# A fused linear-attention and SwiGLU block: tiles 0 to 2 enter K and Q unscaled, GpSimd normalises them, and x 6 to 13 are loaded without a wait

## The chip, the cores and the metric

One core of a Trainium2 chip. The metric is the device time of one execution in microseconds (us), the median of several. Engines are named as in the profile: PE is TensorE (matmuls and transposes), DVE is VectorE, ACT is ScalarE, POOL is GpSimd, SP is SyncE, which here only issues DMAs. Each engine has its own instruction list and works through it in order; a wait at its head holds everything behind it. ACT and SP also have a DMA queue each. SBUF holds 128 partitions; PSUM has eight banks of 128 x 512 f32.

## The reference

x has 2048 rows of 512 bf16 values. `xn` is x less its row mean over its row deviation. The result is `x + A(xn) + B(xn)`:

```
q, k, v = heads of xn @ wqkv            (32 heads of 16)
phi(t)  = where(t > 0, t + 1, exp(t)) + 1e-6
kv = phi(k)^T v,  z = sum of phi(k)     (per head, over all rows)
A  = (phi(q) kv / (phi(q) z + 1e-6)) @ wo
B  = (silu(xn @ w_gate) * (xn @ w_up)) @ w_down      (w_gate, w_up: 512 x 1792)
```

## The kernel before, in words

The rows are cut into 16 tiles of 128. All loads, weights and results lie in SBUF. A small class, `_Prog`, keeps one list per engine. `K.op` appends one entry, with the names that it reads and writes, and puts in the waits that these names need; `K.dma` does it for a DMA. So the order of the calls in the file is the order on each engine.

Stage 1 (lines 537 to 642) goes over the tiles. For tile t: `bns` and `agg` (DVE) give mean and variance; `rstd_pow` gives 1/deviation, an add of 1e-5 (`vpe`, on DVE for the tiles in `VD`, else on POOL) and a pow on POOL; `xn_dve` (DVE) normalises into `xn_sb`; a transpose brings it to `xnT`, from tile 3 on as a DMA transpose on SP's queue; `kproj` and `qproj` (PE, four matmuls of 512 columns each, into banks 2(t mod 2) and 2(t mod 2) + 1); `exp_k`, `exp_q` (ACT, exp of K, exp and copy of Q); `feat_k` (DVE: `clip` to phi's range, then `maxadd`, and on POOL a running sum `zsum`); `gtacc` (PE) accumulates `xn^T phi(k)` into banks 4 to 7. v is never formed: `gtacc`'s sum is multiplied by v's weights later.

The first tiles have their own code. Tile 0 enters the matmuls as x less its mean (`xc_half`, two halves, transposed by PE through PSUM and copied by ACT to `xcT`); since K and Q are linear, rstd is applied as the `scale` of the ACT evictions (`first_ek`, `first_pk`, `first_eq`, `first_pq`), and `first_feat` (DVE) adds relu and clipped exp, both from SBUF. Tiles 1 and 2 are normalised on DVE and transposed by PE. `fill` puts matmuls on constants on PE between these steps.

x 0 to 5 and the weights of K and Q are loaded at the start on both queues (lines 240 to 250). x 6 and 7 are issued on SP behind a wait for the weights of Q (line 251); x 8 to 15 in pairs by `xn(3)`, `xn(5)`, `xn(6)` and `xn(7)`, each right behind that tile's DMA transpose on SP (lines 528 to 535). The later weights follow on SP in the loop at t = 10.

Stage 2 (`ffn`, 56 steps of gate and up matmuls, line 656) has the attention's end woven in, and stage 3 the output matmuls (lines 828 and 839). Neither is touched.

Of the kernel before, what the change touches and what calls it, by code (L numbers as in the profile page):

```python
# [10 lines left out]
P = 128  # L11
S = 2048
D = 512
# [95 lines left out]
def bass_parallel_sum__linear_attn_block__swiglu_ffn__prompt_kernel(  # L109
# [16 lines left out]
    with contextlib.ExitStack() as es:  # L126
# [7 lines left out]
        xc_sb = sb("xc_sb", [D])  # L134
        xcT = sb("xcT", [NDC, P])
        kpos = sb("kpos", [D], f32)
# [103 lines left out]
        xload("sp", sp, 0, 1)  # L240
        xload("sp", sp, 1, 1)
        wqkv_load("act", act, "wk", 1, 0, 2)
        wqkv_load("sp", sp, "wk", 1, 2, 2)
        xload("act", act, 2, 1)
        wqkv_load("act", act, "wq", 0, 0, 2)
        wqkv_load("sp", sp, "wq", 0, 2, 1)
        wqkv_load("act", act, "wq", 0, 3, 1)
        xload("act", act, 3, 1)
        xload("sp", sp, 4, 1)
        xload("act", act, 5, 1)  # L250
        xload("sp", sp, 6, 2, [("wq", 0), ("wq", 2), ("wq", 3)])
# [51 lines left out]
        VD = (1, 2, 3)  # L303
# [34 lines left out]
        def xc_half(h):  # L338
            K.op(
                "dve",  # L340
                lambda: dve.tensor_scalar(
                    out=xc_sb[:, h * HD:(h + 1) * HD], in0=x_sb[:, 0, h * HD:(h + 1) * HD],
                    scalar1=mv[:, 0, 0:1], scalar2=None, op0=ALU.subtract,
                ),
                r=[("x", 0), ("mv", 0)], w=[("xc", h)],
            )

        def xn_half(t, h):
            K.op(
                "dve",  # L350
                lambda: dve.tensor_scalar(
                    out=xn_sb[:, t, h * HD:(h + 1) * HD], in0=x_sb[:, t, h * HD:(h + 1) * HD],
                    scalar1=mv[:, t, 0:1], scalar2=rstd[:, t:t + 1], op0=ALU.subtract, op1=ALU.mult,
                ),
                r=[("x", t), ("mv", t), ("rstd", t)], w=[("xnh", t, h)] + ([("xn", t)] if h else []),
            )

        def transpose_half(src, key, dst, wkeys, b, h):
# [5 lines left out]
                        tb[:, c, :], src[:, (2 * h + c) * P:(2 * h + c + 1) * P], ident[:, :],  # L364
# [3 lines left out]
                r=[key, ("ident",)], w=[bk(b)],  # L368
# [3 lines left out]
                lambda: act.activation(dst[:, 2 * h:2 * h + 2, :], tb, ACT.Copy),  # L372
                r=[bk(b)], w=wkeys,
# [10 lines left out]
        def proj(t, b, lo, wname):  # L384
# [9 lines left out]
                r=[("xnT", t), (wname, 0), (wname, 2)] + ([(wname, 3)] if wname == "wq" else []), w=[bk(b)],  # L394
            )

        def proj_part(src, key, b, lo, wname, h):
# [4 lines left out]
                        banks[b], src[:, c, :], wqkv_sb[:, c, lo:lo + D],  # L402
# [4 lines left out]
                r=[key, (wname, 2 * h)] + ([(wname, 3)] if wname == "wq" and h else []), w=[bk(b)],  # L407
# [48 lines left out]
        def first_ek():  # L456
            K.op(
                "act", lambda: act.activation(ek[:, 0, :], banks[kb(0)], ACT.Exp, scale=rstd[:, 0:1]),
                r=[bk(kb(0)), ("rstd", 0)], w=[("ek", 0)],
            )  # L460

        def first_pk():
            K.op(
                "act", lambda: act.activation(kpos[:, :], banks[kb(0)], ACT.Relu, scale=rstd[:, 0:1]),
                r=[bk(kb(0)), ("rstd", 0)], w=[("kpos",)],
            )

        def first_eq():
            K.op(
                "act", lambda: act.activation(eq[:, 0, :], banks[qb(0)], ACT.Exp, scale=rstd[:, 0:1]),  # L470
                r=[bk(qb(0)), ("rstd", 0)], w=[("eq", 0)],
            )

        def first_pq():
            K.op(
                "act", lambda: act.activation(pkq[:, 0, 1, :], banks[qb(0)], ACT.Identity, scale=rstd[:, 0:1]),
# [459 lines left out]
```

## Time and profile before

| | us |
|---|---|
| median of 3 runs | 212.66 (212.58 to 212.66) |
| profiled execution | 213.16 |
| its span, first to last instruction | 211.9 |
| PE busy in the span | 207.7 (98%) |
| DVE, ACT, POOL busy | 118.9, 68.1, 73.1 |
| K 0's first matmul, line 401 | 5.25 |
| K 3's first matmul, line 388 | 14.10 |
| K 6's first matmul | 22.20 |
| first matmul of stage 2, line 656 | 48.96 |

The granted TensorE clock was 1.000. A row of a timeline gives start, length, engine, line, operation, output<-inputs and, in brackets, how long the engine had been idle and what ended that. Lines are those of the kernel before. A group of several instructions shows the time from the first's start to the last's end. "POOL rstd L316" is the pow, "vpe L309" the add in front of it, "pkq L483" `first_feat`, "zacc" the running sum.

### The profile page before, as it was taken

Reading aid. Unit: us, or ns where it says so; the run is one execution under the profiler, and the core shown is the slowest. Engines: PE = TensorE matmul, PEld = TensorE weight load, DVE = VectorE, ACT = ScalarE, POOL = GpSimd, SP = SyncE. Lnnn points to the kernel's source line nnn. Section 1 sums busy time; section 2 is a strip of 40 time slices with the busy share of each in tenths; the row PEclk is TensorE's granted clock in tenths of the full one; section 3 lists DMA queues with packets and bytes.
Section 4 is the critical chain, followed back from the end, with each engine's and each line's share of the span. In section 5 each row is a group of like instructions: output and inputs, shape, how many; then the busy total and the mean of one; then the engine's idle time right before and its main releaser. Section 6 shows DMA issues by size and latency. Waiting matters only on the chain.

```text
span 211.9 us, 2784 instructions
## 1 busy us (share of the span) xinstructions
PE 207.7 (98%) x1001; PEld 95.9 (45%) x1001; DVE 118.9 (56%) x244; ACT 68.1 (32%) x119; POOL 73.1 (35%) x93
## 2 busy tenths in 40 slices
PE   8899999999999999999999999999999999999996
PEld 3344444445444444444444444444444444444454
DVE  3899796533454776546374746464556535374121
ACT  4486666866453332213122312112032213121000
POOL 3368787748022444122140442131414031221100
PEclk9999999999999999999999999999999999999999
DMA  5647634893792011120101011101021010110201
GB/s 182 214 99 125 152 74 86 282 363 102 200 353 57 0 25 25 50 27 25 47 4 50 10 35 33 50 0 50 3 50 25 25 25 28 45 31 26 51 28 50
DMA packets 28623, 16.45 MB, mean 78 GB/s; under 512 B 19136, under 2 KB 27968, under 8 KB 28608
## 3 DMA queue, kind: packets, MB, share of 16 engines
q1 hardware_dynamic: 27488, 15.21, 27.0%
q10 hardware_dynamic: 1120, 1.05, 1.5%
q8 instruction: 8, 0.13, 0.3%
q14 instruction: 7, 0.06, 0.1%
HBM read 9.70 MB, written 2.10 MB: 56 GB/s over the span
## 4 chain that ended last, share of the span: by engine, by line
PE 89%; DMA 5%; DVE 4%; ACTq 1%; issue 0%; ACT 0%
PE psum L656 46%; PE psum L839 23%; PE psum L388 8%; PE psum L828 7%; PE psum L514 4%; DMA x_sb<-in_A_x_dram 3%; DMA xnT<-xn_sb 2%; DVE stats L288 1%; DVE pkq L450 1%; DVE xn_sb L296 1%; PE psum L754 0%; PE psum L777 0%; ACTq L204 0%; DVE ek L441 0%; DVE pkq L483 0%
## 5 line engine op out<-in xcount | busy, mean ns | idle before, releaser
L671 ACT ACTIVATE sg<-psum 128x512 bf16<-128x512 f32 x56 | 33.4, 598 | 106.8 <-PE psum L656 104.9
L656 PE MATMUL psum<-xnT,wg_sb 128*128 128x512 bf16 x224 | 57.5, 379 | 0.0
L656 PE MATMUL psum<-xnT,wu_sb 128*128 128x512 bf16 x224 | 57.5, 379 | 0.0
L786 POOL TENSOR_TENSOR prod<-pkq,zb 128x512 f32<-128x512 bf16 x16 | 18.6, 1161 | 57.8 <-DVE pkq L450 57.8
L656 PEld LDWEIGHTS psum<-xnT,wu_sb 128*128 128x128 bf16 x224 | 21.9, 98 | 26.4
L656 PEld LDWEIGHTS psum<-xnT,wg_sb 128*128 128x128 bf16 x224 | 21.9, 98 | 26.2
L852 DVE TENSOR_TENSOR out_sb<-psum,x_sb 128x512 bf16<-128x512 f32 (+1 forms) x17 | 11.2, 660 | 36.0 <-PE psum L839 36.0
L677 DVE TENSOR_TENSOR pkq<-psum,sg 128x512 bf16<-128x512 f32 x28 | 19.1, 687 | 18.6 <-PE psum L656 14.0
L810 POOL TENSOR_TENSOR pqn<-pkq,rden 128x512 bf16<-128x512 bf16 x16 | 16.9, 1055 | 36.5 <-DVE rden L804 36.5
L388 PE MATMUL psum<-wqkv_sb,xnT 128*128 128x512 bf16 x116 | 27.3, 379 | 0.2 <-DMA xnT<-xn_sb 0.2
L677 DVE TENSOR_TENSOR xn_sb<-psum,sg 128x512 bf16<-128x512 f32 x28 | 18.8, 672 | 14.2 <-PE psum L656 12.6
L839 PE MATMUL psum<-wd_sb,xn_sb 128*128 128x512 bf16 (+1 forms) x126 | 25.7, 355 | 0.0
L839 PE MATMUL psum<-wd_sb,pkq 128*128 128x512 bf16 x112 | 25.5, 379 | 0.0
L506 POOL TENSOR_TENSOR zacc<-zacc,pkq 128x512 f32<-128x512 f32 x15 | 17.3, 1154 | 6.3 <-DVE ek L441 5.7
L839 PEld LDWEIGHTS psum<-wd_sb,xn_sb 128*128 128x128 bf16 x126 | 12.3, 98 | 11.9
L388 PEld LDWEIGHTS psum<-wqkv_sb,xnT 128*128 128x128 bf16 x116 | 11.1, 98 | 13.9 <-ACT eq L430 0.6
L839 PEld LDWEIGHTS psum<-wd_sb,pkq 128*128 128x128 bf16 x112 | 11.0, 98 | 13.2
L828 PE MATMUL psum<-m_sb,eq 128*128 128x512 bf16 (+1 forms) x68 | 16.6, 366 | 0.0
L514 PE MATMUL psum<-pkq,xn_sb 128*128 128x512 bf16 x64 | 16.1, 379 | 0.0
L794 DVE TENSOR_REDUCE den<-prod 128x32 f32<-128x512 f32 x16 | 10.9, 684 | 5.7 <-POOL prod L786 5.7
L288 DVE BATCH_NORM_STATS2 stats<-x_sb 128x6 f32<-128x512 bf16 x16 | 11.0, 685 | 3.6 <-DMA x_sb<-in_A_x_dram 3.4
L424 ACT ACTIVATE ek<-psum 128x512 bf16<-128x512 f32 x15 | 9.0, 599 | 8.6 <-DVE stats L288 2.1
(67 smaller groups left out, 133.1 us busy)
## 6 DMA issues: line engine op xcount, KB each, us to landing
out_dram<-out_sb SPq DMA_DIRECT2D x15, 128.0 KB, 1.7
wg_sb<-in_B_w_gate_dram SPq DMA_DIRECT2D x2, 896.0 KB, 8.1
wu_sb<-in_B_w_up_dram SPq DMA_DIRECT2D x2, 896.0 KB, 6.1
wd_sb<-in_B_w_down_dram SPq DMA_DIRECT2D x1, 1792.0 KB, 9.7
x_sb<-in_A_x_dram SPq DMA_DIRECT2D x5, 256.0 KB, 3.1
wqkv_sb<-in_A_wqkv_dram ACTq DMA_DIRECT2D x2, 256.0 KB, 4.2
wqkv_sb<-in_A_wqkv_dram SPq DMA_DIRECT2D x1, 512.0 KB, 8.2
wo_sb<-in_A_wo_dram SPq DMA_DIRECT2D x1, 512.0 KB, 9.1
```

Of the source, the lines that this page charges most:

```text
L288: K.op("dve", lambda: dve.bn_stats(stats[:, t, :], x_sb[:, t, :]), r=[("x", t)], w=[("st", t)])
L388: (lambda c=c: pe.matmul(banks[b], xnT[:, c, t * P:(t + 1) * P], wqkv_sb[:, c, lo:lo + D], start=(c == 0), stop=(c == NDC - 1),))
L506: lambda: pool.tensor_tensor(out=zacc[:, :], in0=zacc[:, :], in1=pk, op=ALU.add),
L514: (lambda c=c: pe.matmul(banks[4 + c], xn_sb[:, t, c * P:(c + 1) * P], pkq[:, t, 0, :], start=(t == 0), stop=(t == NT - 1),))
L656: (lambda c=c: pe.matmul(banks[b], w_sb[:, c, fc * P:(fc + 1) * P], xnT[:, c, C * 512:(C + 1) * 512], start=(c == 0), stop=(c == NDC - 1),))
L671: lambda: act.activation(sg[:, j % NSG, :], banks[gb], ACT.Silu),
L677: lambda: dve.tensor_tensor(out=hT(C, fc), in0=banks[ub], in1=sg[:, j % NSG, :], op=ALU.mult,),
L786: lambda: pool.tensor_tensor(out=p, in0=pkq[:, t, 1, :], in1=zb[:, :], op=ALU.mult),
L810: lambda: pool.tensor_tensor(out=pqn[:, t % NPN, :].rearrange("p (h e) -> p h e", e=DH), in0=pkq[:, t, 1, :].rearrange("p (h e) -> p h e", ...
L828: (lambda g=g: pe.matmul(dst, pqnT(t)[:, g, :], m_sb[:, g, lo:hi], start=(g == 0), stop=False,))
L839: (lambda fc=fc: pe.matmul(dst, hT(C, fc)[:, jj * P:(jj + 1) * P], wd_sb[:, fc, lo:hi], start=False, stop=(fc == NFC - 1),))
L852: lambda: dve.tensor_tensor(out=o, in0=src, in1=x_sb[:, t, lo:hi], op=ALU.add),
```

## The change

- Loads: wk comes in three pieces (chunks 0 to 1 on ACT, 2 on SP, 3 on ACT), wq in three (0 to 1 on SP, 2 on ACT, 3 on SP), in a new order on both queues. x 6 to 9 follow on SP and x 10 to 13 on ACT with no wait; x 14 and 15 are issued on ACT at t = 5. The pairs behind `xn(3)` to `xn(7)` are gone.
- Tiles 1 and 2 go as tile 0 did: `xc_half`, PE transposes (`tp_first`), `proj_first`, and the `first_` evictions and adds, now for three tiles, with their own space in `xc_sb`, `xcT` and `kpos`.
- `xn` of tiles 0 to 2, which `gtacc` and stage 2 still need, comes from `xn_pool` on POOL: tile 0's between the statistics of tile 2 and its rstd, tile 1's behind `xn(3)`, tile 2's behind `xn(4)`, both by an added wait.
- All three are brought to `xnT` by DMA transposes at t = 7, 8 and 9.
- K 1 is ahead of Q 0 on PE; `vpe` is on DVE for tiles 3 and 5 only. Fills are 8, 2, 8 and 4 (before: 8, 2, 10 and 3).
- Order: `zsum(0)` directly behind `first_feat(2)`, statistics and normalisations of tiles 3 to 7 and 15 are moved in the list.

```diff
         xload("sp", sp, 0, 1)
+        wqkv_load("act", act, "wk", 1, 0, 2)
         xload("sp", sp, 1, 1)
-        wqkv_load("act", act, "wk", 1, 0, 2)
-        wqkv_load("sp", sp, "wk", 1, 2, 2)
+        wqkv_load("sp", sp, "wk", 1, 2, 1)
+        wqkv_load("act", act, "wk", 1, 3, 1)
         xload("act", act, 2, 1)
-        wqkv_load("act", act, "wq", 0, 0, 2)
-        wqkv_load("sp", sp, "wq", 0, 2, 1)
-        wqkv_load("act", act, "wq", 0, 3, 1)
+        wqkv_load("sp", sp, "wq", 0, 0, 2)
         xload("act", act, 3, 1)
+        wqkv_load("act", act, "wq", 0, 2, 1)
+        wqkv_load("sp", sp, "wq", 0, 3, 1)
         xload("sp", sp, 4, 1)
         xload("act", act, 5, 1)
-        xload("sp", sp, 6, 2, [("wq", 0), ("wq", 2), ("wq", 3)])
+        xload("sp", sp, 6, 4)
+        xload("act", act, 10, 4)
...
-        VD = (1, 2, 3)
+        VD = (3, 5)
...
-        def xc_half(h):
+        def xc_half(t, h):
...
-        def xn_half(t, h):
...
+        def xn_pool(t, after=None):
+            K.op(
+                "pool",
+                lambda: pool.tensor_scalar(
+                    out=xn_sb[:, t, :], in0=x_sb[:, t, :], scalar1=mv[:, t, 0:1], scalar2=rstd[:, t:t + 1],
+                    op0=ALU.subtract, op1=ALU.mult,
+                ),
+                r=[("x", t), ("mv", t), ("rstd", t)] + ([] if after is None else [("xn", after)]), w=[("xn", t)],
+            )
+
+        def tp_first(t, h, b):
...
-        def proj_part(src, key, b, lo, wname, h):
+        def proj_first(t, wname, h):
+            lo, b = (D, kb(t)) if wname == "wk" else (0, qb(t))
...
             if t >= 3:
                 transpose_dma(t)
-            if t == 3:
-                xload("sp", sp, 8, 2)
-            elif 5 <= t < 8:
-                xload("sp", sp, 2 * t, 2)
```

The new order of stage 1, whole, up to the loop:

```
bns(0) agg(0) rstd_pow(0) xc_half(0,0) xc_half(0,1)
bns(1) agg(1) rstd_pow(1) xc_half(1,0) xc_half(1,1)
bns(2) agg(2) xn_pool(0) rstd_pow(2) xc_half(2,0) xc_half(2,1)
fill(8,512) tp_first(0,0,4) fill(2,P) tp_first(0,1,5) fill(8,P)
proj_first(0,wk,0) proj_first(0,wk,1) tp_first(1,0,6) tp_first(1,1,7) fill(4,P)
first_ek(0) first_pk(0) proj_first(1,wk,0) proj_first(1,wk,1) first_ek(1)
proj_first(0,wq,0) tp_first(2,0,4) tp_first(2,1,5) proj_first(0,wq,1)
bns(3) clip(0) agg(3) clip(1) rstd_pow(3) first_feat(0) first_pk(1)
proj_first(1,wq,0) proj_first(1,wq,1) first_eq(0) first_pq(0)
proj_first(2,wk,0) proj_first(2,wk,1) gtacc(0)
xn(3) bns(4) xn_pool(1,3) agg(4) first_feat(1) rstd_pow(4)
first_ek(2) first_eq(1) first_pq(1) first_pk(2)
bns(5) xn(4) xn_pool(2,4) agg(5) proj_first(2,wq,0) proj_first(2,wq,1) gtacc(1)
first_eq(2) first_pq(2) clip(2) rstd_pow(5) first_feat(2) zsum(0)
bns(6) xn(5) agg(6) rstd_pow(6) kproj(3) exp_k(3) qproj(3) exp_q(3)
feat_k(3) stat(7) xn(6) stat(8) gtacc(2)
```

In the loop from t = 4:

```diff
-        XN0 = {4: (7,), 5: (8,), 6: (9,), 7: (10,), 8: (11,), 9: (12, 13), 10: (14, 15)}
-        XN = {}
+        XN0 = {5: (8,), 6: (9,), 7: (10,), 8: (11,), 9: (12, 13), 10: (14,)}
+        XN1 = {4: (7,)}
+        XN = {10: (15,)}
...
+            if t == 5:
+                xload("act", act, 14, 2)
...
             feat_k(t)
+            for i in XN1.get(t, ()):
+                xn(i)
...
-            if t == 7:
-                transpose_dma(0)
+            if t in (7, 8, 9):
+                transpose_dma(t - 7)
```

## The prediction

> **What bounds the kernel now.** I read the page first: TensorE's busy share, then the shares of the chain that ended last. The whole program is one long row of matmuls.
>
> ```profile
> PE 207.7 (98%) x1001; PEld 95.9 (45%) x1001; DVE 118.9 (56%) x244; ACT 68.1 (32%) x119; POOL 73.1 (35%) x93
> PE 89%; DMA 5%; DVE 4%; ACTq 1%; issue 0%; ACT 0%
> ```
>
> The chain in order of time says where the other 11% lie. Columns are start, length and what (us).
>
> ```profile
> 2.93 5.54 DMA x_sb<-in_A_x_dram
> 8.49 0.69 DVE stats L288
> ...
> 17.34 4.73 DMA xnT<-xn_sb
> 22.20 1.89 PE psum L388 x8
> 24.08 0.86 PE psum L514 x4
> 24.95 1.73 PE psum L388 x8
> ```
>
> Up to 22.20 the chain runs through the load of x 3, VectorE and one DMA transpose; from 22.20 (K 6) it is matmuls only. The sizes to see: eight matmuls take 1.73, four 0.86, so 0.216 each, and a tile costs TensorE 2.59 (K, Q and the accumulation of one tile). So the change can gain or lose only by the time at which K 6, with all work ahead of it done, starts. TensorE's own timeline shows the gaps ahead of it.
>
> ```profile
> 5.25 0.59 PE L401 MATMUL psum<-wqkv_sb,xcT 128*128 128x512 bf16 x2
> 6.43 0.59 PE L401 MATMUL psum<-wqkv_sb,xcT 128*128 128x512 bf16 x2 [0.58 <-DMA wqkv_sb<-in_A_wqkv_dram]
> 8.18 0.59 PE L401 MATMUL psum<-wqkv_sb,xcT 128*128 128x512 bf16 x2 [0.30 <-DMA wqkv_sb<-in_A_wqkv_dram]
> 14.10 1.89 PE L388 MATMUL psum<-wqkv_sb,xnT 128*128 128x512 bf16 x8
> 22.20 1.89 PE L388 MATMUL psum<-wqkv_sb,xnT 128*128 128x512 bf16 x8 [0.16 <-DMA xnT<-xn_sb]
> ```
>
> K 0's second half waits for weights, so does Q 0's; from 8.18 the row is dense (K 3 at 14.10) until K 6, which should start at 21.01 + 0.86 = 21.87 and starts 0.33 late: the transpose of tile 6 was issued at 17.34 among loads of x and took 4.73, where the one issued at 11.32 took 2.5. Last, GpSimd and VectorE side by side.
>
> ```profile
> 15.13 0.77 POOL L502 CAST zacc<-pkq 128x512 f32<-128x512 bf16 x1
> 17.41 1.15 POOL L506 TENSOR_TENSOR zacc<-zacc,pkq 128x512 f32<-128x512 f32 x1
> 18.22 0.50 DVE L296 TENSOR_SCALAR xn_sb<-x_sb,mv,rstd 128x512 bf16<-128x512 bf16 x1
> 22.78 0.38 DVE L296 TENSOR_SCALAR xn_sb<-x_sb,mv,rstd 128x512 bf16<-128x512 bf16 x1
> 9.69 0.68 DVE L483 TENSOR_TENSOR pkq<-kpos,ek 128x512 bf16<-128x512 f32 x1
> 9.85 0.93 POOL L316 TENSOR_TENSOR rstd<-vpe,nhalf 128x1 f32<-128x1 f32 x1 [1.75 <-DVE vpe L309]
> 11.77 0.57 POOL L316 TENSOR_TENSOR rstd<-vpe,nhalf 128x1 f32<-128x1 f32 x1
> ```
>
> They hold each other up. A normalisation on VectorE takes 0.38, but 0.50 when it starts inside a GpSimd pass, and then ends 0.16 after that pass (18.72 against 18.56). The pow takes 0.57, but 0.93 when VectorE's add of two SBUF tiles runs: it ends 0.41 after that add. bn_stats (0.69) shows no such thing.
>
> **The change part by part.** Times are profile times; handoffs between engines are 0.03 to 0.11 as in the timeline.
>
> *Weights and order.* Half B of K 0 needs wk 2 and wk 3. On SP's queue 256 KB had landed by 4.56 (the statistic of x 1 starts at 4.58) and 512 KB by 1.72 + 4.6 = 6.3; wk 2 now ends at 384 KB, halfway: 5.5, with 4.6 and 6.3 as bounds. ACT's pieces land by 5.0 (wk 3) and about 6.1 (x 2). Two fewer fills put half A at 5.1 and half B at 5.55 instead of 6.43. Four copies on ACT (0.38, 0.27 apart) behind the transposes of tile 1 let K 1 start at 6.75; Q 0 at 7.6 (its weights stand at the bytes that had landed by 7.4 and 8.05 to 8.25), tile 2's transposes, Q 0's rest 8.3, Q 1 8.7, K 2 9.55, first accumulation 10.45, Q 2 11.3, second accumulation 12.2. Before, that one started at 13.24: TensorE alone is 1.05 ahead, and with the 0.33 of K 6 gone 1.37.
>
> *What must keep up.* VectorE loses 0.41 + 2 x 0.33 + 0.40 of normalising, two vpe (0.15 each) and two max-adds (0.69), and gets four half subtractions (0.285), two adds (0.68) and one vpe: 0.5 less in all. GpSimd gets three normalising passes. None of that size and kind is in the trace. Bounds are its CASTs and its two-input passes: 0.61 (CAST from f32) to 1.16. I take 0.80, next to the CAST that reads one bf16 tile, 0.77, because this pass too reads one bf16 tile. [...]
>
> *The chain through them*, with ek 1 ending at 8.7 on ACT. Pass 0 (6.7 to 7.5) holds tile 2's first subtraction to 7.65, so bn_stats 3, both clips and vpe 3 end at 9.25; the add of tile 0 runs 9.15 to 9.85 and stretches pow 3 as before: 10.25. xn 3 is done at 10.75, its transpose lands 2.5 later: K 3 at 13.3 (14.10 before). Pass 1 waits for xn 3: 10.8 to 11.6. Behind it on GpSimd stand vpe 4 and pow 4. The add of tile 1 (two SBUF inputs) starts at 11.45 and is held to 11.6 + 0.55 = 12.15 (the held normalisation had 0.22 of its 0.38 behind it; I let the add have 0.13 of its 0.68); vpe 4 after it 12.4, pow 4 13.05, xn 4 13.5, landing 16.05: K 4 at 16.1 (16.69). Pass 2: 13.6, held by clip 2 to 13.8, ends 14.5; the add of tile 2 15.1, pow 5 15.5. Then zsum 0 (CAST, 0.77) starts just ahead of xn 5 and holds it to 16.45; landing 18.95: K 5 at 19.0 (19.28). Tile 6's transpose is issued at 18.9 and lands at 21.4, with no load of x around it, so K 6 starts at 19.0 + 2.59 = 21.6 against 22.20. From there TensorE is dense as before. The same steps applied to the kernel before give K 6 at 22.1, 0.1 early, so I take 0.5 of the 0.6.
>
> *Edits taken at nothing.* Seven DMA issues on ACT (0.43 to 0.49 each from 0.94) end at about 4.4, and its first copy starts at 4.64: cover 0.2; one stalled issue would cost that copy and K 0 as much as it exceeds this. x 6 to 13 are 1 MB behind the weights; at the 350 GB/s of 3 to 4 us they end by 11.2, and the transpose issued at 11.32 moved nothing before 12 us (0 GB/s from 11 to 12), so tile 3's, issued at 10.75, hardly meets them. If not, it costs K 3 some tenths, which K 4's own chain already gives away. The late load of x 14 stands on ACT (0.5) between tiles where ACT sits idle 0.7. SP issues two transposes more (1.2 each) and four loads fewer (0.58 each); wg leaves up to 1.3 later, and wu, which landed at 37.43 + 7.2 = 44.6, is read at 49.8: 3 us of cover remain. The extra Relu and scaled evictions (0.69 against 0.60) run on ACT, 0.59 busy in the first 23 us, none last in a wait above.
>
> **Sum.** The profiled execution took 213.16, of which the span is 211.9; 0.5 less makes 211.4 and 212.66. It lies 0.50 above the median of the runs, 212.66, so for the median I forecast 212.15.
>
> **Rivals.**
> *The port does not hold the adds.* The trace shows the add holding GpSimd, and a pass holding a one-input normalisation, never a pass holding an add of two SBUF tiles. If it does not, the adds of tiles 0 to 2 and the pows behind them end on time and TensorE is dense from 12.2: the gain is 1.3 (1.37 less the two fresh handoffs), 211.35. Against it: the 0.93 shows that the two ask for the same thing. [...]
>
> *The passes are dear (slower).* All three lie in the chain: pass 0 delays vpe 3, pass 1 xn 4, pass 2 xn 5. So each 0.1 on a pass costs 0.3 at K 5. The gain is gone at 0.97, and at the two-input rows, 1.06 to 1.16, K 5 comes 0.8 to 1.1 later than above: 0.3 to 0.6 slower, 213.0 to 213.25. For it: two pointer scalars and two operations, where the CAST has none. Against it: one tile read instead of two.
>
> *The key weights land no earlier.* wk 2 at 6.3, as the second half of wk did, delays K 0 half B by 0.75, and with it K 1, ek 1 and the whole chain: 212.6 to 212.9. Against it: half as many bytes stand ahead of it since 4.56. That the free loads crowd the weights is the same rival: they stand behind them on both queues.
>
> **How the numbers follow.** About 0.2% of the time (0.43 us) is what a measurement can tell from no change. Forecast (passes 0.7 to 0.9, held): 0.40, own range 211.8 to 212.5; two thirds of it beyond 0.2%. Free port: 0.22, 211.2 to 211.6. Dear passes: 0.25, a third of it within 0.2%, the rest slower. Late weights: 0.13, half within, half slower or, with a cheap pass, still faster. Faster: 0.26 + 0.22 + 0.02 = 0.50; same: 0.13 + 0.08 + 0.06 = 0.27; slower 0.23. The range 211.2 to 213.2 leaves out the dearest passes with late weights and a little below the free port.
>
> **What would show it.** K 0's second half at 5.5, not 6.4; a normalising pass on GpSimd of 0.7 to 0.9; adds of tiles 1 and 2 of over 0.68; K 3 at 13.3, K 4 at 16.1, K 5 at 19.0 waiting for their transposes, K 6 at 21.6 with no wait; tile 6's transpose at 2.5. Wrong would be: no waits at K 3 to K 5 (free port), a pass above 0.97, a gap at K 0 or Q 0 for weights, or a new gap after 22.

## The result, and the profile after

The changed kernel takes 215.88 us (median of 6 runs, 215.19 to 216.63), beside 212.72 for the kernel before on the same chip: 1.0144 times as long, 95% interval 1.0128 to 1.016. The forecast was 212.15, a gain; it became a loss of 3.1 us (by the ratio; 3.2 by the medians). The profiled execution took 215.19, its span is 213.9 us. In this kernel line 404 is K or Q of tiles 0 to 2, 390 K and Q from tile 3 on, 517 the accumulation, 353 the new normalising pass on GpSimd, 298 the normalisation on VectorE, 486 `first_feat`, 311 `vpe`, 318 the pow, 505 the first copy of the running sum.

The page of the changed kernel, busy times and the chain that ended last:

```profile
PE 208.0 (97%) x981; PEld 96.7 (45%) x1000; DVE 119.9 (56%) x243; ACT 69.8 (33%) x122; POOL 79.0 (37%) x97
...
PE 86%; issue 0%; DVE 0%
```

TensorE's share fell by one point with the same work in it, so the loss is idle time of TensorE, and GpSimd has 5.9 us more to do. TensorE's timeline says where the idle time lies:

```profile
5.80 1.24 PE L404 MATMUL psum<-wqkv_sb,xcT 128*128 128x512 bf16 x4
...
11.44 1.03 PE L517 MATMUL psum<-pkq,xn_sb 128*128 128x512 bf16 x4
...
13.85 1.02 PE L517 MATMUL psum<-pkq,xn_sb 128*128 128x512 bf16 x4 [0.52 <-POOL xn_sb L353]
14.71 1.89 PE L390 MATMUL psum<-wqkv_sb,xnT 128*128 128x512 bf16 x8
...
17.49 1.02 PE L517 MATMUL psum<-pkq,xn_sb 128*128 128x512 bf16 x4 [0.89 <-POOL xn_sb L353]
18.35 1.89 PE L390 MATMUL psum<-wqkv_sb,xnT 128*128 128x512 bf16 x8
...
21.21 1.89 PE L390 MATMUL psum<-wqkv_sb,xnT 128*128 128x512 bf16 x8
...
23.80 1.89 PE L390 MATMUL psum<-wqkv_sb,xnT 128*128 128x512 bf16 x8
...
26.85 1.89 PE L390 MATMUL psum<-wqkv_sb,xnT 128*128 128x512 bf16 x8 [0.29 <-ACT pkq L437]
```

K 0's second half waits for nothing any more, and the first accumulation is where it was (11.44; before 11.51). Then two accumulations wait for the normalised tile that the GpSimd pass writes, K 5 for its transpose (landed at 21.08), and K 7 for its transpose (landed at 26.71; the row names ACT, which had long been done). K 3 comes at 14.71 instead of 14.10, K 6 at 23.80 instead of 22.20, the first matmul of stage 2 at 51.02 instead of 48.96, which is 2.06 later; the profiled executions differ by 2.03, and from there to the end both take 164.2.

The rows of the passes, and VectorE's between them:

```profile
6.63 2.09 POOL L353 TENSOR_SCALAR xn_sb<-x_sb,mv,rstd 128x512 bf16<-128x512 bf16 x1
...
10.05 0.93 POOL L318 TENSOR_TENSOR rstd<-vpe,nhalf 128x1 f32<-128x1 f32 x1 [0.48 <-DVE vpe L311]
11.61 2.09 POOL L353 TENSOR_SCALAR xn_sb<-x_sb,mv,rstd 128x512 bf16<-128x512 bf16 x1 [0.64 <-DVE xn_sb L298]
13.67 0.23 POOL L311 TENSOR_SCALAR vpe<-mv 128x1 f32<-128x1 f32 x1
13.98 0.57 POOL L318 TENSOR_TENSOR rstd<-vpe,nhalf 128x1 f32<-128x1 f32 x1
15.26 2.09 POOL L353 TENSOR_SCALAR xn_sb<-x_sb,mv,rstd 128x512 bf16<-128x512 bf16 x1 [0.71 <-DVE mv L293]
17.31 0.56 POOL L318 TENSOR_TENSOR rstd<-vpe,nhalf 128x1 f32<-128x1 f32 x1
```

```profile
8.53 0.69 DVE L290 BATCH_NORM_STATS2 stats<-x_sb 128x6 f32<-128x512 bf16 x1 [0.86 <-DMA x_sb<-in_A_x_dram]
...
12.16 0.76 DVE L486 TENSOR_TENSOR pkq<-kpos,ek 128x512 bf16<-128x512 f32 x1
...
14.66 0.41 DVE L298 TENSOR_SCALAR xn_sb<-x_sb,mv,rstd 128x512 bf16<-128x512 bf16 x1 [1.14 <-POOL rstd L318]
...
15.45 1.12 DVE L486 TENSOR_TENSOR pkq<-kpos,ek 128x512 bf16<-128x512 f32 x1
...
17.91 0.68 DVE L298 TENSOR_SCALAR xn_sb<-x_sb,mv,rstd 128x512 bf16<-128x512 bf16 x1 [0.74 <-POOL rstd L318]
```

A pass takes 2.09, not 0.80. Behind the second and the third stands the next tile's `vpe` or pow, and VectorE sits idle for it: 1.14 ahead of tile 4's normalisation, 0.74 ahead of tile 5's. That is the chain of the prediction, with a term of 2.09 in two of its three places. The first pass costs nothing: it ends at 8.72, VectorE waits for x 3 until 8.53, and GpSimd sits idle for 0.48 before the pow of tile 3.

### The profile page after: what moved, and what is told of

Same layout as the page of the kernel before. It is cut to its first block, busy times and chain, and to the rows that moved or that the text cites. A ratio compares the mean times of both kernels' runs of the same rounds, so it can differ in the third digit from the quotient of the medians.

```text
span 213.9 us, 2775 instructions
## 1 busy us (share of the span) xinstructions
PE 208.0 (97%) x981; PEld 96.7 (45%) x1000; DVE 119.9 (56%) x243; ACT 69.8 (33%) x122; POOL 79.0 (37%) x97
## 4 chain that ended last, share of the span: by engine, by line
PE 86%; issue 0%; DVE 0%
PE psum L675 45%; PE psum L858 23%; PE psum L390 7%; PE psum L847 6%; PE psum L517 4%; PE psum L773 0%; PE psum L796 0%; DVE out_sb L871 0%
## 5 line engine op out<-in xcount | busy, mean ns | idle before, releaser
L675 PE MATMUL psum<-xnT,wg_sb 128*128 128x512 bf16 x217 | 56.0, 379 | 0.4
L871 DVE TENSOR_TENSOR out_sb<-psum,x_sb 128x512 bf16<-128x512 f32 (+1 forms) x17 | 11.2, 660 | 36.0 <-PE psum L858 36.0
L390 PE MATMUL psum<-wqkv_sb,xnT 128*128 128x512 bf16 x103 | 24.3, 379 | 0.5 <-ACT pkq L437 0.3
L390 PEld LDWEIGHTS psum<-wqkv_sb,xnT 128*128 128x128 bf16 x104 | 10.0, 98 | 13.1 <-ACT pkq L437 0.8
L453 DVE SCALAR_TENSOR_TENSOR pkq<-pkq,eq 128x512 bf16<-128x512 bf16 x16 | 11.1, 692 | 0.6
```

The source lines that it names most:

```text
L390: (lambda c=c: pe.matmul(banks[b], xnT[:, c, t * P:(t + 1) * P], wqkv_sb[:, c, lo:lo + D], start=(c == 0), stop=(c == NDC - 1),))
L453: lambda: dve.scalar_tensor_tensor(out=dst, in0=src, scalar=0.0, in1=e, op0=ALU.max, op1=ALU.add,),
L675: (lambda c=c: pe.matmul(banks[b], w_sb[:, c, fc * P:(fc + 1) * P], xnT[:, c, C * 512:(C + 1) * 512], start=(c == 0), stop=(c == NDC - 1),))
L871: lambda: dve.tensor_tensor(out=o, in0=src, in1=x_sb[:, t, lo:hi], op=ALU.add),
```

## Experiments

The theory after this reading: the passes are dear by their form, and cost by their length; the loads of x without a wait crowd Q's weights. Rivals came up on the way and stand with each run. By the front I mean all of stage 1 up to K 3, and by cover the time by which something is there before it is needed. The kernel before ran beside each of them: 212.72 to 212.92 in the median, 213.40 beside the last pair.

**What a GpSimd instruction costs.** Eight instructions at the end of the kernel before, where GpSimd has nothing to do; the output is untouched.

```diff
+        tsc(scr[:, :], x0, m0, r0, ALU.subtract, ALU.mult)      # the pass
+        tsc(scr[:, 0:256], x0[:, 0:256], m0, r0, ALU.subtract, ALU.mult)
+        tsc(scr[:, :], x0, m0, None, ALU.subtract, None)
+        tsc(scr[:, :], x0, 0.5, 2.0, ALU.subtract, ALU.mult)
+        tsc(scr[:, :], x0, 0.5, None, ALU.mult, None)
...
+        K.op("pool", lambda: pool.tensor_copy(scr[:, :], x0), w=[("scr",)])
+        K.op("pool", lambda: pool.tensor_tensor(out=scr[:, :], in0=x0, in1=r0.broadcast_to([P, D]), op=ALU.mult), w=[("scr",)])
```

> The kernel before, with eight GpSimd instructions on 512 columns of bf16 added behind its last step of stage 2, where GpSimd has nothing left to do and nobody waits for it: subtract and multiply with two per-partition scalars, the same on 256 columns, with one per-partition scalar, with two constants, with one constant, with an f32 output, a plain copy, and a multiply by a broadcast tensor. Theory (the form itself costs 2.09): the first reads 2.05 to 2.10, the one on 256 columns about half plus a fixed 0.2 (1.15), the broadcast multiply 1.05 as the other two-input rows. Rival (2.09 comes from company, VectorE and the loads holding the port at that place): the first reads 0.7 to 1.2 here. Time: within 0.2% of the kernel before.

The view of that tile, durations in ns (smallest, median, largest):

```profile
L909 POOL TENSOR_SCALAR scr<-x_sb,mv,rstd x2: 1232/1663/2094, 197.2 to 199.4; 128x512 bf16<-128x512 bf16 x1, 128x256 bf16<-128x256 bf16 x1
L911 POOL TENSOR_SCALAR scr<-x_sb,mv x1: 1564/1564/1564, 200.7 to 200.7; 128x512 bf16<-128x512 bf16 x1
L909 POOL TENSOR_SCALAR scr<-x_sb x1: 1927/1927/1927, 202.4 to 202.4; 128x512 bf16<-128x512 bf16 x1
L911 POOL TENSOR_SCALAR scr<-x_sb x1: 1497/1497/1497, 204.4 to 204.4; 128x512 bf16<-128x512 bf16 x1
L922 POOL COPY scr<-x_sb x1: 609/609/609, 208.1 to 208.1; 128x512 bf16<-128x512 bf16 x1
L925 POOL TENSOR_TENSOR scr<-x_sb,rstd x1: 1041/1041/1041, 208.8 to 208.8; 128x512 bf16<-128x512 bf16 x1
```

With nothing beside it but one add on VectorE that reads PSUM (0.69), the pass takes 2094 ns; on 256 columns it takes 1232, so by these two 3.37 ns a column and 0.37 us besides. One operation instead of two saves 0.53, constants in place of pointers 0.17. The price is that of the instruction, not of its company. The product with rstd, which reads two tensors, costs half: what I had called the upper bound (two inputs) is the cheaper form of the two.

**The passes moved to VectorE.** The same three calls at the same places:

```diff
         def xn_pool(t, after=None):
             K.op(
-                "pool",
-                lambda: pool.tensor_scalar(
+                "dve",
+                lambda: dve.tensor_scalar(
```

> The changed kernel with the three normalising passes on VectorE (0.38 each) at the same places of the order. Theory (the passes' price sets K 3 to K 7): the second accumulation at 13.2 to 13.3 without a wait for GpSimd, K 4 at 17.1 instead of 18.35, first matmul of stage 2 about 1.6 earlier, so 214.0 to 214.5 against 215.88. Rival (the loads without a wait crowd the weights and x 3, and that is the loss): no more than 0.3 better, 215.5 or above.

214.17 (213.37 to 215.23), 1.0052 times the kernel before (1.0027 to 1.0076): 1.7 of the 3.1 are back. What TensorE still waits for up to 30 us, by the view of waits:

```profile
PE psum L404 <- DMA wqkv_sb<-in_A_wqkv_dram: 0.8, 1, 0.8
PE psum L390 <- DMA xnT<-xn_sb: 0.4, 1, 0.4
```

The waits for POOL are gone. Q 0 waits for its first weights (landed at 8.64, where the prediction had 7.4), K 6 for its transpose.

**Half the pass.** The same place on GpSimd, in the cheaper form (the centred tile times rstd):

```diff
-                lambda: pool.tensor_scalar(
-                    out=xn_sb[:, t, :], in0=x_sb[:, t, :], scalar1=mv[:, t, 0:1], scalar2=rstd[:, t:t + 1],
-                    op0=ALU.subtract, op1=ALU.mult,
+                lambda: pool.tensor_tensor(
+                    out=xn_sb[:, t, :], in0=xc_sb[:, t, :], in1=rstd[:, t:t + 1].broadcast_to([P, D]), op=ALU.mult,
```

> The changed kernel with each of the three GpSimd passes as a product of the centred tile and rstd, two tensors in, at 1.04 us instead of 2.09. Theory 'length': the passes cost by how long GpSimd is taken, since the pow of the next tile and the accumulation stand behind them. Then halving them gives most of the 1.7 us back that moving them to VectorE gave: 214.1 to 214.9, with the waits of the second and third accumulation for the normalised tile (0.52 and 0.89) gone or below 0.2. Rival 'place': GpSimd is the wrong place whatever the length (its handoffs, the shared access to SBUF): 215.4 or more.

214.49 (213.13 to 215.44), 1.0073 (1.0049 to 1.0097): 1.4 better than the changed kernel. No accumulation waits for POOL in its trace, and K 3 starts at 13.52. Its profile then loses the most to a transpose, that of tile 7, which met the load of x 14 and 15 and a 16 KB transfer that is told of below, and took 5.2:

```profile
26.39 1.89 PE L389 MATMUL psum<-wqkv_sb,xnT 128*128 128x512 bf16 x8 [1.75 <-DMA xnT<-xn_sb]
```

In the medians half the length gives back most of what taking the pass away gives: length, not place.

**Who holds whom.** Five pairs at the end of the kernel before, GpSimd's pass started together with a row of VectorE instructions.

```diff
+        beside(1, p_pass, v_add, 4)     # pass 2.09, adds of two SBUF tiles
+        beside(2, p_pass, v_norm, 6)    # normalisations
+        beside(3, p_pass, v_stat, 3)    # bn_stats
+        beside(4, p_mul, v_add, 3)      # product 1.04
+        beside(5, p_copy, v_norm, 4)    # copy 0.61
```

> The kernel before with five pairs at its end, where GpSimd and VectorE are idle: GpSimd runs one pass while VectorE runs a row of one kind. Measures how long VectorE's instructions are held. (1) normalising pass of 2.09 beside four adds of two SBUF tiles (0.68 alone); (2) the same beside six normalisations (0.38 alone); (3) beside three bn_stats (0.69); (4) the product of 1.04 beside three adds; (5) a copy of 0.61 beside four normalisations. As forecast before (held for the whole pass): in (1) the first add ends 0.55 after the pass's end. As read from the changed kernel's trace: only the first 0.7 us of the normalising pass hold VectorE, so the first add ends about 1.2 to 1.4 after the pass's start, and the second runs at 0.68 inside it; in (4) and (5) the hold lasts to the pass's end; in (3) nothing is held.

Pairs 1, 2 and 4 in the timelines of GpSimd and VectorE:

```profile
197.56 3.14 POOL L915 TENSOR_SCALAR scr<-x_sb,mv,rstd 128x512 bf16<-128x512 bf16 x1
...
200.81 2.19 POOL L915 TENSOR_SCALAR scr<-x_sb,mv,rstd 128x512 bf16<-128x512 bf16 x1
...
205.76 1.58 POOL L920 TENSOR_TENSOR scr<-x_sb,rstd 128x512 bf16<-128x512 bf16 x1
```

```profile
197.61 2.91 DVE L926 TENSOR_TENSOR vtt<-kpos,xn_sb 128x512 bf16<-128x512 f32 x4 [1.40 <-POOL tick L910]
200.79 2.67 DVE L929 TENSOR_SCALAR vts<-x_sb,mv,rstd 128x512 bf16<-128x512 bf16 x6 [0.27 <-POOL tick L910]
...
205.75 2.74 DVE L926 TENSOR_TENSOR vtt<-kpos,xn_sb 128x512 bf16<-128x512 f32 x3 [0.21 <-POOL tick L910]
```

The four adds took 0.69, 0.68, 1.10 and 0.68: only the third was held, by 0.42, and the pass itself was stretched from 2.08 (beside bn_stats) to 3.14. Beside normalisations it was stretched by 0.1, and two of the six took 0.70 and 0.75. bn_stats was not held, nor held anything. The product of 1.04 grew to 1.58 and held the second add to 1.53, to 0.55 after the product's end. My own reading had the first add held and the second free; it was the third, and why is not shown: the pass had started 0.05 ahead of the first add. In the changed kernel, where the adds of tiles 1 and 2 came 0.55 and 0.19 into a pass, the pass kept its 2.09. So "held for the whole pass", as forecast, fits the product and the copy (which held a normalisation to 0.66, 0.15 past the copy's end) and not the pass: only single instructions beside it were held, and in the first pair the adds held it up more (1.06) than it did them.

**The loads of x without a wait, alone in the kernel before.**

```diff
-        xload("sp", sp, 6, 2, [("wq", 0), ("wq", 2), ("wq", 3)])
+        xload("sp", sp, 6, 4)
+        xload("act", act, 10, 4)
...
-            if t == 3:
-                xload("sp", sp, 8, 2)
-            elif 5 <= t < 8:
-                xload("sp", sp, 2 * t, 2)
+            if t == 7:
+                xload("sp", sp, 14, 2)
```

> The kernel before with x 6 to 13 loaded with no wait as in the change, nothing else. Theory (passes): the late start of K 6 (0.33) goes, the weights of Q and x 3 land up to 0.8 later and give a part of it back: 212.3 to 213.1. Rival (crowding): the whole chain behind x 3 and Q 0 moves by 0.7 or more, 213.4 or above.

213.66 (213.35 to 214.02), 1.003 (1.0015 to 1.0045): 0.6 slower by the ratio, 0.9 by the medians. TensorE's timeline:

```profile
8.42 0.59 PE L402 MATMUL psum<-wqkv_sb,xcT 128*128 128x512 bf16 x2 [0.56 <-DMA wqkv_sb<-in_A_wqkv_dram]
...
10.71 0.40 PE L326 MATMUL psum<-ident,xn_sb 128*128 128x128 bf16 x4 [0.83 <-DVE xn_sb L297]
```

x 3 landed at 9.62 instead of 8.46, and VectorE, whose next statistic waits for it, was late with tile 2. So crowding, the rival, is what happened in this kernel. The loads stand behind the weights in each queue, but their packets did not wait for all of the weights': in the trace of the changed kernel the 4 KB packets of x 6 on ran from 7.5 us, while the 1 KB packets ahead of them in the queues, wq's among them, ran to 9.2.

**The wait put back in the changed kernel**, with the passes still on GpSimd, and then with the passes on VectorE:

```diff
-        xload("sp", sp, 6, 4)
-        xload("act", act, 10, 4)
+        xload("sp", sp, 6, 4, [("wq", 0), ("wq", 2), ("wq", 3)])
+        xload("sp", sp, 10, 4)
```

> The changed kernel with x 6 to 13 put behind the weights of Q, both loads on SP; the passes stay on GpSimd. Theory (passes): x 3 and the weights of Q land 0.5 to 0.8 earlier, but ek 1 and the passes end the chain, so 0 to 0.4 better, 215.5 to 215.9. Rival (crowding): 1 us or more better, 214.9 or below.

> The changed kernel with the three passes on VectorE and x 6 to 13 on SP behind a wait for Q's weights: both suspects taken out at once. Theory: slow passes and free loads are nearly the whole loss. Q 0 starts at 7.8 instead of 8.7, K 3 at 13.2 to 13.4, and the time is 212.8 to 213.5; what it may still lie above the kernel before is that K 0 now runs while TensorE has not yet reached full speed, which the wait for weights hid before. Rival: the new order and the unscaled entry of tiles 1 and 2 cost by themselves: 213.9 or more, as with the passes on VectorE alone (214.17).

215.57 (1.0101, 1.005 to 1.0153) and 214.58 (1.0072, 1.0042 to 1.0102). The first is as expected; the second is not: with both suspects out it is no better than with the passes alone on VectorE (214.17). So passes and free loads are not the whole, and what the loads cost in the kernel before does not add up with the rest. In this trace x 0 landed at 3.69 instead of 3.00, K 3 started at 14.50, and K 6 waited 1.22 for its transpose, which took 4.1 us.

**What made a transpose take 4 us.** The kernel before with all of x behind the weights and no load among the transposes:

```diff
-        xload("sp", sp, 6, 2, [("wq", 0), ("wq", 2), ("wq", 3)])
+        xload("sp", sp, 6, 5, [("wq", 0), ("wq", 2), ("wq", 3)])
+        xload("sp", sp, 11, 5)
...
-            if t == 3:
-                xload("sp", sp, 8, 2)
-            elif 5 <= t < 8:
-                xload("sp", sp, 2 * t, 2)
```

> The kernel before with x 6 to 10 and 11 to 15 in two loads right behind the wait for Q's weights, and no load between the transposes. This tells what made the transpose of tile 6 take 4.73 us. Theory 'code': a 16 KB transfer of the instruction queue at 19.2 us slowed the packets around it, not the loads of x; then tile 6's transpose still takes 3.4 us or more although no load of x is near it. Rival 'loads': the transposes are slowed by loads of x alone; then it takes 2.5. By both the loads end by 13.3, tile 3's transpose meets their end and is some 0.0 to 0.5 later, and K 6 loses its wait of 0.33: 212.3 to 212.9.

212.92, the same as before (1.0006, 0.9992 to 1.002). What I call the code transfer, a 16 KB packet on the instruction queue, came at 25.58 here and missed tile 6, whose transpose took 2.54; the one of tile 9, issued at 23.06, met it and took 3.3. The DMA view of two stretches says it side by side, first of the kernel with its passes on VectorE (18.5 to 20.6 us, the transpose of tile 6, no load of x in it), then of this one (16.4 to 19.5 us):

```profile
q8 instruction: 1, 0.02, 3.3%
...
xnT<-xn_sb SPq DMA_TRANSPOSE x1, 3.7
```

```profile
q1 hardware_dynamic: 1088, 0.26, 41.9%
...
xnT<-xn_sb SPq DMA_TRANSPOSE x3, 2.4
```

A code transfer with no load beside it lengthened a transpose from 2.5 to 3.3 here, 3.7 in the kernel with its passes on VectorE, and 4.1 in the changed kernel (tile 9). A load of x does it too: in the profile before, whose code transfer ran at 19.2, the transposes issued at 13.43 and 21.88, each right behind a load of 256 KB, took 2.9 and 3.1. The first code transfer came anywhere from 19.2 to 28.4 us in these traces; what sets its time no run shows. It also corrects my reading of the profile before: its wait of 0.33 at K 6 was one execution's bad luck. This kernel never shows it and is no faster in the median.

**The rest, by the order of the work.** Three kernels with the passes on VectorE. The first has x 10 to 15 behind the weights, none in the loop; the second also moves, on VectorE, the statistics and `vpe` of tiles 3 and 4 ahead of the clip of tile 1, tile 1's normalisation into the idle time ahead of x 3, tiles 5 and 6 ahead of the adds; the third has x 10 to 15 in threes behind the transposes of tiles 3 and 5.

```diff
-        xload("sp", sp, 10, 4)
+        xload("sp", sp, 10, 6)
...
-            if t == 5:
-                xload("act", act, 14, 2)
```

> The changed kernel with the passes on VectorE, x 6 to 9 and then 10 to 15 on SP behind the wait for Q's weights, and no load of x in the loop. Apart from the last load it is the kernel that took 214.58. Theory 'load in the loop': what is left above the kernel before is the transposes of tiles 6 and 7, which have no more than 0.4 us of cover and meet the load of x 14 and 15; then it takes 213.4 to 213.9 and K 7 waits for nothing. Rival 'order': what is left is VectorE's order, in which vpe of tile 3 stands behind the clip of tile 1 and so behind K 1 and its exp, so that every late start at the front comes through to K 6; then this kernel takes 214.2 to 214.8 still.

214.11 (1.0056, 1.0019 to 1.0094), between the two. In its profile K 7 waits for nothing, but K 3 starts at 15.54: x 0 was late (3.78) and TensorE reached full speed only at 9.0 (the four matmuls of 512 columns from 6.56 took 1.91, the six from 9.17 took 1.47).

```diff
-        VD = (3, 5)
+        VD = (3, 4, 5)
...
         xc_half(2, 1)
+        xn_pool(1)
...
+        clip(ek[:, 0, :], ("ek", 0))
         bns(3)
-        clip(ek[:, 0, :], ("ek", 0))
         agg(3)
-        clip(ek[:, 1, :], ("ek", 1))
         rstd_pow(3)
...
+        xn(6)
         feat_k(3)
...
-        xn(6)
```

> As the one above, with another order on VectorE: statistics and vpe of tiles 3 and 4 ahead of the clip of tile 1, tile 1's normalisation in the idle time ahead of x 3's landing, normalisations of tiles 5 and 6 ahead of the adds, the running sum's first copy behind them. Theory 'order': the transposes of tiles 3 to 6 are issued 0.3 to 1 us earlier against their K, the waits for them go, TensorE is dense from Q 0 on, K 6 starts at 21.0 to 21.5 (22.20 before) and the time is 212.0 to 212.8, with runs less far apart. Rival 'front': the time was lost ahead of K 1 (TensorE not yet at full speed, the landing of x 0) and no order behind it brings it back: 213.5 or more.

214.15 (1.0042, 1.0014 to 1.0069). The time is the rival's, but its account does not fit: in the profile the first accumulation came at 10.43, where the prediction had 10.45, and the gain was lost again at once behind it.

```profile
10.43 1.03 PE L517 MATMUL psum<-pkq,xn_sb 128*128 128x512 bf16 x4
...
12.66 1.04 PE L517 MATMUL psum<-pkq,xn_sb 128*128 128x512 bf16 x4 [0.34 <-DVE pkq L486]
14.45 1.90 PE L390 MATMUL psum<-wqkv_sb,xnT 128*128 128x512 bf16 x8 [0.75 <-DMA xnT<-xn_sb]
```

Tile 3's transpose was issued at 10.62 behind 1.25 MB of x on the same queue and took 3.8, not 2.5. From 10.5 to 12 this queue moved 105 packets, and 16 of them were under 512 B; two transposes of the changed kernel moved 1088 of that size (18 to 24 us, no load beside them).

```diff
-        xload("sp", sp, 10, 6)
...
+            if t == 3:
+                xload("sp", sp, 10, 3)
+            elif t == 5:
+                xload("sp", sp, 13, 3)
...
+        clip(ek[:, 1, :], ("ek", 1))
+        first_feat(1)
         bns(4)
         agg(4)
         rstd_pow(4)
-        clip(ek[:, 1, :], ("ek", 1))
-        first_feat(1)
```

> The kernel with the new order on VectorE, with x 10 to 12 loaded behind tile 3's transpose and x 13 to 15 behind tile 5's (only x 6 to 9 directly behind Q's weights), and the add of tile 1 ahead of the statistics of tile 4. In the one before it the transpose of tile 3 stood on SP's queue behind 1.25 MB of x and took 3.78 us, and K 3 waited 0.75 for it, the second accumulation 0.34 for the add. Theory 'last waits': these two were what ate the earlier front. Then the transpose takes 2.5, K 3 starts at 13.1 to 13.6, K 6 at 21.0 to 21.6, the profiled run is at 212.2 to 212.8 and the median 212.4 to 213.3, no slower than the kernel before. Rival 'front': in the median the gain is lost ahead of K 1 by runs in which x 0 lands late or TensorE reaches full speed late: 213.4 or more, although the waits are gone.

214.01 (1.0053, 1.004 to 1.0067). K 3 was at 13.56, as expected, but the time is not: the waits came up again at the next two accumulations, of tiles 2 and 3:

```profile
PE psum L516 <- DVE pkq L452: 0.7, 1, 0.7
PE psum L516 <- DVE pkq L485: 0.5, 1, 0.5
```

**The changed kernel once more**, to tell its own waits from one execution's (no edit).

> The changed kernel again, unchanged, for a second profile. To see which of its waits belong to it and which to one execution. Expected of both theories: the second accumulation waits 0.4 to 0.9 for GpSimd's pass, the third 0.8 to 1.0, passes 2.09. Theory 'front': the time at which TensorE reaches full speed, or x 0's landing, differs from the first profile's, and the first accumulation (11.37 to 11.6 before and after so far) differs by as much.

215.97. Its front is another one:

```profile
5.16 1.03 PE L404 MATMUL psum<-wqkv_sb,xcT 128*128 128x512 bf16 x4
...
6.77 1.04 PE L404 MATMUL psum<-wqkv_sb,xcT 128*128 128x512 bf16 x4
...
8.79 0.60 PE L404 MATMUL psum<-wqkv_sb,xcT 128*128 128x512 bf16 x2 [0.98 <-DMA wqkv_sb<-in_A_wqkv_dram]
...
17.26 1.02 PE L517 MATMUL psum<-pkq,xn_sb 128*128 128x512 bf16 x4 [0.90 <-POOL xn_sb L353]
...
25.02 1.89 PE L390 MATMUL psum<-wqkv_sb,xnT 128*128 128x512 bf16 x8 [1.29 <-DMA xnT<-xn_sb]
```

K 0 at 5.16 and K 1 at 6.77 are the prediction's 5.1 and 6.75, 0.6 to 0.9 earlier than in the first profile. Then Q 0 waits 0.98 for its weights, so that the first accumulation comes at 11.81, later than in the first profile and not earlier; the third accumulation waits for the pass as in the first profile, the second no longer (it is late anyway), and K 6 loses 1.29 to a transpose that met a code transfer and the start of the load of x 14. The total is 0.8 worse for all the better start.

**VectorE's order mended once more**, for the two waits that the third order had left.

```diff
         xn_pool(2)
+        first_feat(2)
         xn(5)
-        first_feat(2)
...
-        xn(6)
         feat_k(3)
+        xn(6)
...
-        XN0 = {5: (8,), 6: (9,), 7: (10,), 8: (11,), 9: (12, 13), 10: (14,)}
-        XN1 = {4: (7,)}
-        XN = {10: (15,)}
+        XN0 = {4: (7,), 5: (8,), 6: (9,), 7: (10,), 8: (11,), 9: (12, 13), 10: (14, 15)}
+        XN1 = {}
+        XN = {}
```

> As the kernel whose second accumulation came at 12.69, with VectorE's order mended where its waits had moved to: the add of tile 2 ahead of tile 5's normalisation, tile 3's clip and add ahead of tile 6's normalisation, which there waited idle for its pow, and tile 7's normalisation ahead of the clip of tile 4. In that kernel these two adds held the third and fourth accumulation for 0.52 and 0.66. Theory 'waits move on': VectorE's order was what was left; TensorE is dense from Q 0 to the end of the front, K 6 starts at 21.2 to 21.9 (22.85 there), and the median is 212.3 to 213.2. Rival 'front': something in the new front costs about 1 us in most executions without showing as a wait behind Q 0: 213.5 or more.

213.92 (213.16 to 214.97), 1.0037 (1.0019 to 1.0055): still 1.0 slower than before. K 3 started at 14.02 in the profile, where TensorE was at half speed to 6.4 (the four matmuls of 512 columns from 5.79 took 1.32, where four at full speed take 1.03), and three waits of 0.2 to 0.4 are left:

```profile
PE psum L516 <- DVE pkq L452: 0.4, 1, 0.4
PE psum L389 <- ACT pkq L436: 0.3, 1, 0.3
PE psum L389 <- DMA xnT<-xn_sb: 0.2, 1, 0.2
```

**Two single parts in the kernel before.** The new order of the weights (the edit is that of the change, x 6 and 7 still behind the wait), and tile 6's normalisation later:

```diff
-        xn(6)
         feat_k(3)
         stat(8)
+        xn(6)
```

> The kernel before with the changed kernel's pieces and order of the loads of wk, wq and x 0 to 5; x 6 and 7 still wait for Q's weights, everything else as before. Theory 'order of loads': K 0's second half no longer waits to 6.4 (5.5 to 6.1), but Q's first weights land at 7.8 to 8.3 instead of 7.4 and hold Q 0's first half, which here started at 7.28, so nothing is left at Q 1 and the time is 212.8 to 213.4. Rival: the order is a gain that the rest of the change threw away: 212.0 to 212.6.

> The kernel before with tile 6's normalisation, and so its transpose and the load of x 12 behind it, issued behind the clip and add of tile 3 and the statistics of tile 8, some 1.2 us later, at 18.5, about where the changed kernel with its passes on VectorE issued it (18.62). Theory 'cover': the changed kernels issue the transposes of tiles 6 and 7 2.9 to 3.4 us ahead of their use instead of 4.5, and an execution in which a code transfer or a load of x meets them pays the difference: 213.0 to 213.6 with runs further apart. Rival: 1.2 us of cover are to spare: 212.6 to 212.9.

213.48 and 213.72 beside 213.40: 1.0012 (0.9983 to 1.004) and 1.0006 (0.9981 to 1.003). Neither differs from the kernel before by more than its interval, which reaches to a loss of 0.4% (0.9 us). The kernel before stood 0.5 to 0.7 higher in this pair than beside the other runs, so the times expected can't be compared as they stand. The first is instructive: K 0 ran through from 5.77 without a wait, and Q 0's second half waited 0.73 instead, to 8.94. The wait for the weights had moved from K to Q, and no time was won. The second leaves the theory of lost cover unproven: its profile, of the fastest of its runs, shows no wait for a transpose, and moved alone, tile 6's transpose had the time to spare there.

**All profiles side by side.** "Full rate" is when matmuls of 512 columns go from 0.43 to 0.216 apart, or those of 128 columns from 0.106 to 0.057 (where TensorE sat idle over that time, its next matmul). "Idle" is the first matmul of stage 2 less the start of K 3, less 34.54, which is the dense row between them (3 x 2.592, and the 26.76 from K 6 to stage 2 of the kernel before). From stage 2 on all take 164.1 to 164.3, but for the kernel of the five pairs with its longer end. Each profile is of one execution, some of them at an end of their runs: 213.37, 213.44 and 215.19 are the fastest of theirs, 214.02 the slowest.

| kernel | profiled time | full rate from | K 3 | stage 2 | idle |
|---|---|---|---|---|---|
| before | 213.16 | 3.8 | 14.10 | 48.96 | 0.32 |
| before, eight instructions at the end | 212.90 | 3.7 | 13.77 | 48.67 | 0.36 |
| before, five pairs at the end | 224.47 | 3.7 | 13.85 | 48.99 | 0.60 |
| before, tile 6 later | 212.60 | 4.7 | 13.89 | 48.44 | 0.01 |
| before, all x behind the weights | 212.67 | 4.9 | 13.96 | 48.50 | 0.00 |
| before, x without a wait | 214.02 | 4.3 | 15.26 | 49.79 | 0.0 |
| before, new order of weights | 214.52 | 5.2 | 14.78 | 50.39 | 1.07 |
| changed | 215.19 | 6.2 | 14.71 | 51.02 | 1.77 |
| changed, second profile | 215.97 | 4.3 | 14.47 | 51.78 | 2.77 |
| changed, x behind the weights | 216.02 | 6.4 | 14.78 | 51.86 | 2.54 |
| changed, half passes | 214.72 | 5.2 | 13.52 | 50.56 | 2.50 |
| passes on VectorE | 213.37 | 4.7 | 14.10 | 49.22 | 0.58 |
| and x behind the weights | 214.89 | 6.5 | 14.50 | 50.74 | 1.70 |
| and no load in the loop | 214.66 | 9.0 | 15.54 | 50.41 | 0.33 |
| second order | 213.44 | 3.7 | 14.45 | 49.18 | 0.19 |
| third order | 214.09 | 5.2 | 13.56 | 49.86 | 1.76 |
| last order | 214.21 | 6.4 | 14.02 | 50.06 | 1.50 |

The kernel before has K 3 at 13.77 to 14.10 in the four profiles with its front unchanged. The new front brings it to 13.5 at best, 0.25 to 0.6 earlier, and only where TensorE is at full rate by 5.2 and the weights of Q are there; otherwise to 14.0 or later. Where it does come earlier (half passes, third order), the row behind it is idle for 1.8 to 2.5. No profile has both an early K 3 and a dense row.

## Why the prediction was wrong

**The step that failed: "None of that size and kind is in the trace. Bounds are its CASTs and its two-input passes: 0.61 ... to 1.16. I take 0.80."** It measured 2.09, nearly twice the upper bound, and above the 0.97 that the prediction had named as a sign of being wrong. The reason I gave, that the pass "reads one bf16 tile", bounds nothing here: the form with two scalars and two operations costs twice the form with two tensors, and 3.4 times the copy, which reads one bf16 tile too (2094 against 609 ns). So the rival "the passes are dear" is what happened, beyond its range. Its rule (gain gone at 0.97, 0.3 at K 5 for each 0.1) would give 212.66 + 11.2 x 0.3 = 216.0 for 2.09, beside 215.88 measured, but the agreement is luck: taking the passes away gave back 1.7 and not 3.4. "All three lie in the chain" was wrong too: the first pass cost nothing, because the statistics of tile 3 waited for x 3 anyway.

**"They stand behind them on both queues."** Wrong, a second loss. The free loads cost the kernel before 0.6 to 0.9 by themselves. In the changed kernel Q's weights landed at 8.31, 9.22 and 9.03, where the prediction had 7.4, 8.05 and 8.25. There the wait put back brought 0.3 in the median, within the runs' spread, so this share of the 3.1 is not settled.

**The port "held" for a whole pass.** Wrong for this pass (0.42 of 3.14 in the measured pair); the adds of tiles 1 and 2 took 0.76 and 1.12, the first near its forecast (0.70). The port is my name for whatever the two engines share; no run shows what that is, only which rows grew. It decided nothing: what VectorE and the accumulations waited for in the profile were the pow and the pass, not the adds.

**The weights of K, and the front.** Right where TensorE is at full rate: wk landed by 5.33 (5.5 forecast), and the second profile has K 0 and K 1 where the prediction put them; the second order's first accumulation came at 10.43 against 10.45. Not in the prediction: in the first profile TensorE was at half rate until 6.2 (K 0's second matmul came 0.43 after its first, the two behind it 0.215 apart), K 0 started at 5.80 and K 1 at 7.63. In the kernel before this would cost little, because K 0's second half waited for weights until 6.1 to 6.5 in five profiles out of six; but that is argued, since none of them had so late a full rate. If so, the wait that the change removes was cover for it.

**"With the 0.33 of K 6 gone."** A mistake of the base. The 0.33 belonged to the profiled execution, which stood 0.50 above the median; I took it as a gain and then took the 0.50 off as well. The kernel without that wait has the median of the kernel before.

**"Tile 6's transpose ... lands at 21.4, with no load of x around it."** It took 2.45 in the first profile, as forecast, and 4.2 in the second, where a code transfer and the start of a load met it; tile 7's took 3.7 among x 14 and 15.

**Taken at nothing, rightly:** the DMA issues on ACT, the late wg and wu, stage 2; behind stage 2's start nothing differs by more than 0.1.

**What stays open.** Of the 3.1, the passes are 1.7 by the kernel with them on VectorE. With the loads behind the weights and three orders on VectorE, 1.0 to 1.7 of loss remain by the medians. The table shows that it is idle time ahead of stage 2, and each profile names another wait for it: Q's weights, an add on VectorE, a transpose. That they are one thing, too little cover behind an earlier front, is argued and not shown: the one run that took cover away alone (tile 6 later) showed no loss clear of its interval. A rival is left in the table: full rate came after 6 us in five of the ten profiles with the changed front (in two of them x 0 had landed late), and in none of the seven of the kernel before and its variants (5.2 at the latest). Up to 4.3 us TensorE's list is the same in both, so this may be chance; no run settles it. The unscaled entry of tiles 1 and 2 and K 1 ahead of Q 0 were not tried alone. No version beat the kernel before.

## What to carry to other kernels

Price an instruction by a row of its own form on its own engine; "one input, same tile" is no bound, and eight instructions at the idle end of a kernel give the price in one run. A wait that you remove may have been cover for something that varies from run to run, and what is gained ahead of a row counts only if every later feeder of that row (adds, weights, transposes) has as much slack as the gain. Take a stall of one profiled execution as a gain only once, and not if the execution stands that far above the median.

## What the runs showed of the hardware that I had not expected

- GpSimd's tensor_scalar on 128 x 512 bf16: 2.09 us with two scalars from memory, 1.93 with two constants, 1.56 and 1.50 with one operation; the product of two tensors took 1.04, a copy 0.61.
- GpSimd's pass and VectorE's adds of two SBUF tiles held each other up: 2.08 grew to 3.14, one add of four from 0.68 to 1.10.
- TensorE started at half rate (0.43 for 512 columns) and reached 0.216 at 3.7 to 9.0 us after the span's start, at other times in other executions, while the profile's rows gave the granted clock as 1.00 from the first microsecond.
- A 16 KB transfer on the instruction queue, at 19.2 to 28.4 us, lengthened a DMA transpose beside it from 2.5 us to between 3.3 and 4.1. A transpose issued behind 1.25 MB of loads on the same queue took 3.8 instead of 2.5, and to 1.4 us after its issue the queue had moved 16 packets under 512 B, where two transposes have 1088.
- Loads issued behind others on two queues overtook them in part: packets of 4 KB ran from 1.7 us ahead of the end of earlier 1 KB packets in the changed kernel, and in the kernel before with these loads an earlier load of x landed 1.2 later.
